# A fused attention and FFN kernel on one core: the order table of its steps, its engine lists and its buffer slots laid out anew

## The chip, the core and the metric

The kernel runs on one core of a Trainium2 chip. Five instruction streams run beside each other and meet through semaphores: PE (TensorE, matrix products), DVE (VectorE), ACT (ScalarE), POOL (GpSimd) and SP (SyncE, which here only issues DMAs). Each works through its own instructions in order. The metric is the device time of one launch in microseconds; a shorter time is better.

## What is computed

Two blocks follow each other. The first is a polynomial-sketch attention over 4 batches, 4 heads, 1088 positions and head size 32; the second is a multiplicative feed-forward block on the 4352 rows of 128 that come out of it.

```
phi(x):  a = x @ S1.T ; b = x @ S2.T            # 8 + 8 features
         phi = outer(a, b) flattened            # 64 features
kv  = sum_s phi(k)[s] v[s] ;  z = sum_s phi(k)[s]
x   = (phi(q) @ kv) / (phi(q) @ z + 1e-6)       # heads side by side: 4352 x 128
h   = ((x @ w1) * (x @ w2)) @ w3                # 4352 x 1024
out = h @ w_out                                 # 4352 x 128, float32
```

The four weights arrive as float64 and are put together from their 32-bit words on the chip. The kernel never forms `h`: it multiplies `w3 @ w_out` once (`w3o`, 1024 x 128) and computes `out = ((x@w1)*(x@w2)) @ w3o`.

## The kernel before

The kernel is a set of 1179 named steps, each a few lines that issue one to sixty-four instructions. A table, `ORDER`, names every step once, and the program is recorded in that order; so each engine's queue is `ORDER` with the steps of the other engines taken out. Three more tables belong to it: `POOL` names the steps whose elementwise work goes to POOL instead of DVE, `CPV` the copies that go to DVE instead of ACT, and `SLOTS` says for five kinds of buffers which slot each new tile takes (`b`: the eight PSUM banks). A tile that takes a slot again waits for the last reader of the tile that held it.

The steps by name, with the lines of the profile:

- `s.*`: the sketch matrices. `s.Pp` (L409 to L412) makes three 32x32 blocks of their squares.
- `k0.*` to `k3.*`, one per batch: `lead`/`rest` split the keys into a leading and a lower part (ACT L211, L212 or DVE; L651), `gram0` to `gram4` form the 32x32 Gram matrices (PE, L659: 72 fp32 products per batch, four heads on four column strips of the array), `T`, `N` (L883 to L912) turn these into the denominator's factors, `kv` (L769) sums phi(k) v, `kp` makes phi(k) (L677).
- `q0`, `q1`, `q2`, `q3`, `q4`, `q6`, `qr`: one group of query rows each. For `q0`: `sma`, `sta`, `sha`, `sla`, `sca` and the same with `y` (L1074, L201, L204, L1097, L1101) split small products into a high and a low part, `al` (L1170) adds them up, `p01`, `p2`, `p12`, `dn`, `de`, `rc` make the reciprocal of the denominator, `phi0`, `phi1` (L1208) the features, `x0`, `x1` the product with kv, `xs`, `xt` spread the reciprocal, `xT0`, `xT1` (L1291) give the first group of 512 columns of `x` transposed. `q1.sm`, `st`, `sh`, `sl`, `Ct` are the next group's split (L1137, L201, L204, L1157, L1130).
- `w0` to `w10`: eleven blocks of 1 MB of weights: `load` (SP), `c` and `m` (ACT), `j` (DVE), `a0`, `a1` (POOL). `f0` to `f7`: `t` (DVE) and `m` (PE, L534) build `w3o`.
- `g0` to `g3`: the FFN on groups of 512 columns. For each of eight slices `c`: `a` and `b` (PE, L1799 and L1809, 128x128 times 128x512), `c` (a copy out of PSUM), `m` (DVE, the product), `o` (PE, L1835).
- `h4` and `h6`: groups 4 and 5, and 6 and 7, as a seven-product Strassen-like scheme. `h4.0a1` to `h4.3b7` (PE, L1673) use half the rows of the array each: `a` steps rows 0 to 63, `b` steps rows 64 to 127. `h4.0P1` to `h4.3P7` (PE, L1759) use half the columns each. `m`, `T`, `k` are the elementwise steps around them.
- `gr`: the last 256 columns, with `a`, `b` as above (256 columns wide) and `o` (L1824, 128 wide). `g0.oT` and `g0.st` and their like turn a result and store it (four DMAs on SP).

What sets the order of the work is thus `ORDER` alone, with the waits of data and of slots. `UNDER_WAY` lets a bulk load start only when the bulk load four before it has landed.

Of the kernel before, what the change touches and what calls it, by code (L numbers as in the profile page):

```python
# [78 lines left out]
k1.zero s.Pm warm5 q0.l1 q0.A0 warm6 kr0.ab k0.lead1 q0.rm q0.sma q0.sta warm7 k0.kT0 v0.load v0.loadr k1.load k0.ab1  # L79
q0.sha k0.rest1 q0.C0 k0.gram1 k0.gram2 k0.gram3 k0.gram4 k0.ab0 k0.abc1 q1.max q0.C0t q0.sla q1.l2 k1.loadr s.Pp  # L80
k0.Gm k0.Gt k0.Ga w1.c1 k0.Gb k0.abc0 k0.T0 q1.l1 warm8 kr0.abc k0.kp1 q0.sca w1.j1 k0.Ta k0.kp0 k0.Gc w1.c0 k1.tr0
kr1.load k2.zero k1.tr1 k1.kT1 kr0.kp warm9 k0.N0 warm10 k0.Na warm11 k0.T1 k0.kv0 k0.Tc k0.Tb k0.N1 k0.Nb k0.Nh q1.rm
q0.al k0.Nf q0.phi0 q0.phi1 q0.A1 q0.smy w1.m1 k1.max q0.sty q0.shy k0.kv3 k0.kv1 k0.kv2 q0.sly s.KS k0.kvr kr1.tr
k0.kvm w1.m0 kr1.kT q0.p01 q1.C0 q1.C1 q0.C1 k0.kzt k2.loadr q0.pt0 q0.C1t q0.scy q0.p2 k0.kz q0.pt1 k0.kvc kr1.ab
k0.kqt q0.p12 q0.dn q0.de q0.rc w1.j0 q0.pc0 q0.pc1 q0.x0 k1.kT0 q0.x1 q0.xs0 q0.xs1 q0.xt0 w1.a0 q1.A0 k2.load
w0.load k1.lead0 q0.xc0 q0.xc1 k0.kq w1.a1 k2.max q0.xt1 k1.ab q0.xT0 q0.xT1 g0.4a q1.load g0.5a q1.sm w0.m1 q1.st
# [1848 lines left out]
```

## Time and profile before

| | |
|---|---|
| time of one launch, median of 3 runs | 245.70 us (245.46 to 246.02) |
| span of the profiled execution, first to last instruction | 244.1 us |
| what lies around the span, by the median | 1.6 us |
| granted TensorE clock over the span | 0.998 |
| HBM read and written | 19.40 MB and 2.23 MB |

The profiled execution has no launch time of its own beside its span, so the 1.6 us between the span and the median stands for what lies around it.

The profile is read by engine: a row of a timeline gives the start, the length, the engine, the line of the kernel, the operation, output and inputs, and in square brackets how long the engine stood idle before it and what ended that. A row for a stretch of time gives each engine's busy time in it with the number of instructions, the granted clock and the DMA share. PE and PEld are the products and the weight loads of one and the same engine. An fp32 product leaves two records of products and two of weight loads, a transposition one of each.

### The profile page before, as it was taken

Reading aid. Unit: us, or ns where it says so; the run is one execution under the profiler, and the core shown is the slowest. Engines: PE = TensorE matmul, PEld = TensorE weight load, DVE = VectorE, ACT = ScalarE, POOL = GpSimd, SP = SyncE. Lnnn points to the kernel's source line nnn. Section 1 sums busy time; section 2 is a strip of 40 time slices with the busy share of each in tenths; the row PEclk is TensorE's granted clock in tenths of the full one; section 3 lists DMA queues with packets and bytes.
Section 4 is the critical chain, followed back from the end, with each engine's and each line's share of the span. In section 5 each row is a group of like instructions: output and inputs, shape, how many; then the busy total and the mean of one; then the engine's idle time right before and its main releaser. Section 6 shows DMA issues by size and latency. Waiting matters only on the chain.

```text
span 244.1 us, 6745 instructions
## 1 busy us (share of the span) xinstructions
PE 236.2 (97%) x2724; PEld 129.8 (53%) x2724; DVE 206.7 (85%) x421; ACT 123.5 (51%) x246; POOL 161.9 (66%) x203
## 2 busy tenths in 40 slices
...
GB/s 201 265 143 325 181 227 190 6 197 224 220 141 251 188 217 190 59 1 3 3 0 0 4 0 3 59 113 3 1 0 0 0 3 0 0 1 3 12 90 93
DMA packets 31935, 22.06 MB, mean 90 GB/s; under 512 B 21280, under 2 KB 26528, under 8 KB 31904
## 3 DMA queue, kind: packets, MB, share of 16 engines
...
q8 instruction: 21, 0.34, 0.6%
...
HBM read 19.40 MB, written 2.23 MB: 89 GB/s over the span
## 4 chain that ended last, share of the span: by engine, by line
PE 87%; DMA 5%; ACT 2%; POOL 2%; DVE 1%; issue 1%; POOLq 0%; SPq 0%
PE b_ps L1809 12%; PE ps_o L1835 12%; PE ps_X L1673 11%; PE a_ps L1799 11%; PE ps_o L1759 10%; PE ps_w3o L534 6%; PE ps_Y L1673 6%; PE ps_Z L1673 3%; PE ps_g L659 2%; PE ps_x L1527 2%; PE ps_ac L1374 2%; DMA qh<-in_q_dram 2%; DMA k<-in_k_dram 2%; PE ps_or L1824 2%; POOL ph L1208 1%; PE idle_ps L255 1%
## 5 line engine op out<-in xcount | busy, mean ns | idle before, releaser
L1673 PE MATMUL ps_X<-xd,wv 64*128 64x512 f32 x112 | 36.3, 593 | 0.0
L1799 PE MATMUL a_ps<-xT,w 128*128 128x512 f32 (+1 forms) x80 | 36.1, 562 | 0.0
L1809 PE MATMUL b_ps<-xT,w 128*128 128x512 f32 (+1 forms) x80 | 35.6, 555 | 0.0
L1804 ACT COPY ffa<-a_ps 128x512 f32<-128x512 f32 (+1 forms) x38 | 20.1, 540 | 29.2 <-PE a_ps L1799 26.7
L1707 POOL TENSOR_TENSOR hc<-hc 128x512 f32<-128x512 f32 x16 | 20.7, 1304 | 15.7 <-DVE hc L1685 15.5
L1835 PE MATMUL ps_o<-ab,w3o 128*128 128x512 f32 x64 | 29.6, 600 | 0.0
L1680 ACT COPY hc<-ps_X 128x512 f32<-128x512 f32 x38 | 21.3, 590 | 16.1 <-PE ps_X L1673 12.9
L1815 DVE TENSOR_TENSOR ab<-ffa,b_ps 128x512 f32<-128x512 f32 (+1 forms) x40 | 23.9, 623 | 4.9 <-PE b_ps L1809 4.1
L501 POOL TENSOR_TENSOR w3c<-w3c,cv_m 128x512 int32<-128x512 int32 x16 | 21.2, 1344 | 4.2 <-DVE w3c L495 4.1
L1673 PEld LDWEIGHTS ps_X<-xd,wv 64*128 64x128 f32 x112 | 14.9, 186 | 13.1 <-issue 10.9
L1799 PEld LDWEIGHTS a_ps<-xT,w 128*128 128x128 f32 x80 | 14.1, 189 | 13.9 <-issue 8.8
L1809 PEld LDWEIGHTS b_ps<-xT,w 128*128 128x128 f32 x80 | 14.4, 190 | 13.1 <-issue 8.1
L1673 PE MATMUL ps_Y<-xd,wv 64*128 64x512 f32 x48 | 19.7, 594 | 0.0
L1835 PEld LDWEIGHTS ps_o<-ab,w3o 128*128 128x128 f32 x64 | 11.6, 190 | 13.4 <-issue 13.0
L534 PEld LDWEIGHTS ps_w3o<-wo,w3T 128*128 128x128 f32 x128 | 15.3, 192 | 2.4 <-issue 2.4
L534 PE MATMUL ps_w3o<-wo,w3T 128*128 128x128 f32 x128 | 15.7, 276 | 0.0
L1759 PE MATMUL ps_o<-hc,w3o 128*64 128x512 f32 x32 | 15.1, 595 | 0.0
L1759 PE MATMUL ps_o<-tt,ws 128*64 128x512 f32 x32 | 13.7, 594 | 0.0
L1680 ACT COPY hc<-ps_Y 128x512 f32<-128x512 f32 x14 | 8.1, 592 | 9.7 <-PE ps_Y L1673 6.6
L263 ACT ACTIVATE cv_c<-raw 128x1024 f32<-128x1024 f32 (+1 forms) x13 | 13.0, 1014 | 0.0
L1540 ACT COPY xd<-ps_x 64x256 f32<-64x256 f32 x24 | 8.8, 367 | 7.2 <-PE ps_o L1835 6.8
...
## 6 DMA issues: line engine op xcount, KB each, us to landing
...
```

What stands on the lines that cost most here:

```text
L263: act.activation(dst, hi.bitcast(F32), ACT.Prelu, scale=2.0 ** -112, alpha=-2.0 ** 32)
L501: pool.tensor_tensor(d, d, x["m"][:, i * 512:(i + 1) * 512], ALU.add)
L534: pe.matmul(t["o"], w3T[ko][:, c], wo[:, c], start=c == 0, stop=c == NC - 1)
L1673: pe.matmul(x[bank], stat(j, u)[:, i * 128:(i + 1) * 128], rows(j, u), start=new, stop=True, tile_position=(u * 64, 0), skip_group_check=True)
L1680: cp(n(y))(x[k], x[bank])
L1707: on(f"h{g}.{i}m{k}").tensor_mul(both[0][k], both[0][k], both[1][k])
L1759: pe.matmul(acc_o[bank][half[0]:half[1]], w(i), x(i), start=n == 1, stop=n == (2 if j == 3 else 4), tile_position=(0, half[0]), skip_group ...
L1799: pe.matmul(x["a"][:, :w], w_of(0, c), xT[g][:, c0:c0 + w], start=True, stop=True)
L1804: cp(f"g{g}.{c}{su}c")(x["s"][:, :w], x["a"][:, :w])
L1809: pe.matmul(x["b"][:, :w], w_of(1, c), xT[g][:, c0:c0 + w], start=True, stop=True)
L1815: dve.tensor_mul(ab_sb[g, c][:, c0:c0 + w], x["s"][:, :w], x["b"][:, :w])
L1835: pe.matmul(o_ps[g], w3o[:, c], ab_sb[g, c], start=n == 1, stop=n == NC)
```

## The change

All code below the tables is the same; the tables `ORDER`, `SLOTS`, `POOL` and `CPV` are replaced, so every step still runs once and issues what it issued. Of the 1179 steps the first 60 stand as they stood (to `q0.sma`); behind them the order is another one. The steps in `POOL` rise from 90 to 97 (27 leave it, 34 come to it), those in `CPV` from 17 to 21. One table line more moves every line below by one (L1673 becomes L1674).

```diff
 POOL = set("""
...
-    h6.1m22 h6.2T1 h6.2T4 h6.2m11 h6.3T3 h6.3m11 h6.s1 h6.s2 h6.s4 k0.Nf k0.Nh k0.Nr k0.kp1 k1.Nr
-    k1.kp1 k2.kp0 k2.kp1 k2.rest0 k3.kp0 k3.kp1 q0.al q0.p01 q0.phi1 q0.sca q1.al q1.bs q1.p12
...
-    qr.p12 qr.p2 s.KS s.Pp s.blk s.blkh s.low s.rest
...
+    k0.Nr k0.kp1 k1.Nr k1.kp0 k1.kp1 k2.Nr k2.kp0 k2.kp1 k2.rest0 k3.Nr k3.kp0 k3.rest0 q0.p01
+    q0.p12 q0.phi0 q0.phi1 q1.al q1.bs q1.p12 q1.p2 q1.phi q1.sca q1.scy q2.bs q2.p12 q2.sl q3.al
...
 ORDER = """
...
-h4.0ah h4.1bc h4.0b6 h4.0be h4.0a6 h4.s4 h4.0ae h4.0bh h4.1a6 h4.1b6 h4.1be h4.0b3 h4.1ad h4.1ae h4.0a5 h4.0ad g1.st
...
+h4.1a1 g2.oT h4.0b1 o.S4 qr.xT0 g1.oT h4.0a1 h4.s3 h4.0ac o.S3 h4.0b5 h4.0a2 h4.0b2 h4.s2 h4.1a5 h4.1ac h4.s4 h4.0a6
+h4.1a6 h4.0bc h4.0b6 h4.0ah h4.1b1 h4.0bd h4.0bh h4.0be v.4 h4.1ae h4.0b3 h4.0ae h4.0a5 h4.0b7 h4.1ad h4.0a7 h4.0ad
```

Among the steps of `h4` and `h6`, those of the form `h4.0a2` or `h4.0b2` are PE's half products: `a` on rows 0 to 63 of the array, `b` on rows 64 to 127. Before, a run of one half is one or two long, and wherever the 112 of them are cut into pairs from the start of a stretch, each pair holds one of each half. Now the table has runs of three as well: from `h4.0a2` on it reads a, b, a, a, a, b, b, b. In the column halves of `h6` there are two such runs.

Three places, row by row. First DVE, from the split of the low sums of `q0` (the first row, `s_t<-s_gy`, is `q0.sty`) to the first columns of `x`. Before:

```order
L201 SCALAR_TENSOR_TENSOR s_t<-s_gy,ps_ay 128x128
L204 SCALAR_TENSOR_TENSOR s_hiy<-s_gy,s_t 128x128
L1097 TENSOR_TENSOR s_loy<-ps_ay,s_hiy 128x128
L1068 STREAM_TRANSPOSE ay_C_601<-ps_cy 128x128
L1101 TENSOR_TENSOR s_loy<-s_loy,ay_C_601 128x128
L1180 TENSOR_TENSOR s_pr<-s_al,s_loy 128x128
L1184 TENSOR_TENSOR s_pr<-s_pr 128x128
L1189 TENSOR_REDUCE s_d<-s_pr 128x2x16
L1194 SCALAR_TENSOR_TENSOR s_rc<-s_d 128x16
L1198 RECIPROCAL s_rc<-s_rc 128x16
L466 TENSOR_SCALAR w_81<-cv_c 128x2x256
L1274 COPY xc<-ps_xt 128x256 x2
```

Of the change, where `s_g`, `s_t_598`, `s_hl` and `ay_C<-ps_c` are the split of `q1`:

```order
L202 SCALAR_TENSOR_TENSOR s_t<-s_gy,ps_ay 128x128
L202 SCALAR_TENSOR_TENSOR s_t_598<-s_g,ps_a 128x256
L205 SCALAR_TENSOR_TENSOR s_hiy<-s_gy,s_t 128x128
L205 SCALAR_TENSOR_TENSOR s_hl<-s_g,s_t_598 128x2x128
L1069 STREAM_TRANSPOSE ay_C_606<-ps_cy 128x128
L1098 TENSOR_TENSOR s_loy<-ps_ay,s_hiy 128x128
L1102 TENSOR_TENSOR s_loy<-s_loy,ay_C_606 128x128
L1181 TENSOR_TENSOR s_pr<-s_al,s_loy 128x128
L1158 TENSOR_TENSOR s_hl<-ps_a,s_hl 128x2x128
L1131 STREAM_TRANSPOSE ay_C<-ps_c 128x384
L1190 TENSOR_REDUCE s_d<-s_pr 128x2x16
L1195 SCALAR_TENSOR_TENSOR s_rc<-s_d 128x16
```

The split of `q1` moved ahead of the reciprocal of `q0`, into the places between its steps; `q0.p12` (L1184) left for POOL.

Second PE, between the Gram matrices of batch 1 and those of batch 2 (`ps_T`, `ps_N` are `k1.T`, `k1.N`, `ps_ph` the transpositions of `q1.pt`, `ps_x` is `q1.x`). Before:

```order
L1799 MATMUL a_ps<-xT,w_81 128x512
L889 MATMUL ps_T<-RS,G_a 32x32
L890 MATMUL ps_T<-RS,G_c 32x32
L891 MATMUL ps_T<-RS,G_b 32x32
L1246 MATMUL ps_ph<-ident,ph 128x128 x4
L1799 MATMUL a_ps<-xT,w_81 128x512 x2
L1809 MATMUL b_ps<-xT,w_81 128x512
L1246 MATMUL ps_ph<-ident,ph 128x128 x4
L1809 MATMUL b_ps<-xT,w_81 128x512
L912 MATMUL ps_N<-T_p,P2a 32x8 x4
L912 MATMUL ps_N<-T_p,P2b 32x8 x4
L912 MATMUL ps_N<-T_p,P2s 32x8 x8
```

Of the change, from `k2.ab` (`ps_ab`) on:

```order
L728 MATMUL ps_ab<-kT,KS 32x256 x8
L913 MATMUL ps_N<-T_p,P2a 32x8 x4
L913 MATMUL ps_N<-T_p,P2b 32x8 x4
L913 MATMUL ps_N<-T_p,P2s 32x8 x8
L1247 MATMUL ps_ph<-ident,ph 128x128 x4
L1800 MATMUL a_ps<-xT,w_81 128x512 x2
L1247 MATMUL ps_ph<-ident,ph 128x128 x4
L1810 MATMUL b_ps<-xT,w_81 128x512
L1298 MATMUL ps_x<-pT,kz_658 64x512 x2
```

Before, `k1.N` is followed by `q1.x` and at once by 72 Gram products; now the transpositions and three products of `g0` stand between `k1.N` and them, and `k2.ab` has come ahead of both.

Third PE, from the last column-half products of `h6` to the last products of all. Before:

```order
L1824 MATMUL ps_or<-w3o,ab 128x128 x3
L1759 MATMUL ps_o<-hc,ws 64x512 x2
L1824 MATMUL ps_or<-w3o,ab 128x128
L1799 MATMUL a_ps<-xT,w_81 128x256
L1809 MATMUL b_ps<-xT,w_81 128x256
L1759 MATMUL ps_o<-hc,ws 64x512 x2
L1799 MATMUL a_ps<-xT,w_81 128x256
L1824 MATMUL ps_or<-w3o,ab 128x128
L1809 MATMUL b_ps<-xT,w_81 128x256 x3
L1799 MATMUL a_ps<-xT,w_81 128x256
L1824 MATMUL ps_or<-w3o,ab 128x128
L1809 MATMUL b_ps<-xT,w_81 128x256
```

Of the change:

```order
L1760 MATMUL ps_o<-tt,w3o 64x512
L1810 MATMUL b_ps<-xT,w_81 128x256
L1800 MATMUL a_ps<-xT,w_81 128x256
L1825 MATMUL ps_or<-w3o,ab 128x128 x2
L1800 MATMUL a_ps<-xT,w_81 128x256
L1825 MATMUL ps_or<-w3o,ab 128x128
L1800 MATMUL a_ps<-xT,w_81 128x256
L1810 MATMUL b_ps<-xT,w_81 128x256 x2
L1825 MATMUL ps_or<-w3o,ab 128x128
L1810 MATMUL b_ps<-xT,w_81 128x256 x2
L1825 MATMUL ps_or<-w3o,ab 128x128 x12
```

All column-half products (L1759, now L1760) now stand in one piece ahead of `gr`'s products; before, two pairs of them stood among these, and one pair of row halves (L1673) between six products of `gr` and the first column halves.

More of the change, by code (lines that the diff above doesn't have):

```diff
@@ L78 @@
 warm3 s.rest w1.load s.T s.P s.tc warm4 q0.l2 k0.kT1 s.Pc s.R k0.g k0.lead0 s.c s.blk k0.rest0 q1.tr k0.gram0 s.blkh
[L79 to L86, printed above, removed]
-q1.Ct g0.4c g0.4b q1.sh q1.sl k1.rest0 g0.7b w0.c1 g0.7a k1.abt w0.j1 k1.gram0 w0.c0 s.RC q1.scy k1.gram1 kh2.load
@@ L98 @@
-q2.x q2.load k2.N0 k2.Tb k3.lead0 w9.a1 k2.N1 g1.4b q3.al q3.p2 q3.p12 q2.xT0 g2.5a k3.kT1 g2.5c g2.6a q3.dn q3.de
-k2.Na g1.3m g2.4a g2.3a w5.m g2.4b g2.6c k3.rest0 g1.0b k2.Nr q3.rc g1.1m g1.4m g1.6b k2.Nb g0.2b kr1.kp w6.j q4.tr
-g2.4c g1.6m w7.load w7.c q3.bs q4.max q2.restT w6.m w5.j w2.j q4.l2 w3.load w9.a0 k3.gram0 k3.gram1 k3.gram2 q3.load
-w7.j q3.phi0 k3.gram3 k3.gram4 g2.2a k3.Gc g2.1a g1.0m w2.a0 g2.6b g2.0a g2.4m g2.1c f6.t w6.a0 w4.load g2.3b w2.a1
-g2.2b g2.2c g2.0c w6.a1 g2.1b q3.pT0 k3.Gm g0.2m k3.Gt k3.kT0 v3.load w7.m f6.m w5.a1 w5.a0 g2.3c k3.Ga k3.Gb g2.3m
@@ L138 @@
[L138 to L142 removed]
+k1.zero s.Pm warm5 q0.l1 q0.A0 warm6 kr0.ab k0.lead1 q0.rm q0.sma v0.load k0.ab1 s.Pp q0.C0 k0.gram1 kr0.abc k0.kT0
@@ new lines @@
+q0.sta q1.max kr1.load q0.sha k0.rest1 kr1.tr k0.abc1 k0.ab0 k0.gram2 k0.gram3 k1.load q0.C0t q1.l2 k0.gram4 q0.sla
+k1.loadr k1.tr1 w0.load k0.Gm q1.l1 warm7 warm9 q0.sca kr0.kp k0.Gt k0.Ga k0.Gc k0.kp1 q0.al k0.T0 k1.max k2.zero
+k0.Gb k0.Ta k0.T1 k0.Tc k2.loadr k0.Tb kr1.kT k1.tr0 k0.N0 k0.abc0 q1.rm k0.Na w1.m1 s.KS k0.N1 q0.phi0 k1.kT1 k0.Nh
+w1.c0 w1.m0 warm10 q0.pt0 q0.A1 k1.kT0 warm11 kr1.ab q1.A0 k0.Nb v0.loadr k0.Nf q1.C0 k0.kp0 q0.smy k0.kv0 k0.kv3
+w0.c0 q0.C1 k0.kv1 q1.C1 w1.c1 w6.load w0.m0 q1.sm q0.sty w0.c1 q1.st q0.shy q1.sh q0.phi1 q0.C1t kh2.load k0.kv2
```

143 lines of the change are left out of this document (76 added, 67 removed).

## The prediction

> **What bounds the kernel now.** I read the page's engine line first, then the busy time by stage, then the chain that ended last.
>
> ```profile
> span 244.1 us, 6745 instructions
> PE 236.2 (97%) x2724; PEld 129.8 (53%) x2724; DVE 206.7 (85%) x421; ACT 123.5 (51%) x246; POOL 161.9 (66%) x203
> ```
> ```profile
> core 0: us, PE busy (x) PEld busy (x) DVE busy (x) ACT busy (x) POOL busy (x), PEclk, DMA share, GB/s
> 15.00:27.42 12.42, 11.17 (x256) 8.63 (x256) 9.99 (x34) 9.26 (x22) 6.83 (x11) 1.00 0.68 215
> 27.42:49.10 21.68, 20.28 (x454) 10.99 (x454) 19.12 (x46) 15.05 (x30) 13.60 (x18) 1.00 0.63 152
> 49.10:155.70 106.60, 106.60 (x1369) 59.60 (x1364) 94.21 (x196) 56.24 (x108) 76.12 (x67) 1.00 0.39 97
> 155.70:240.60 84.90, 84.86 (x401) 39.63 (x400) 75.11 (x122) 33.03 (x63) 56.96 (x69) 1.00 0.14 24
> ```
>
> The second column of numbers is PE. From 49.10 to 240.60 us it is never idle (106.60 of 106.60, 84.86 of 84.90), and the clock column stands at 1.00. There an order can only win by giving PE less to do between its products, and can lose by making PE wait. Up to 49 us PE does wait: 1.40 us in the row that starts at 27.42, and more before it, where it fills its time with idle products. The share of 97% hides this. So three places are worked out: the start of the first FFN product, the waits up to 49 us, and the joints between kinds of products later.
>
> The joints can be read in the chain of the last stretch (start, length, line, records).
>
> ```profile
> 218.99 0.43 PE b_ps L1809 x2
> 219.42 1.06 PE ps_X L1673 x4
> 220.48 10.45 PE ps_o L1759 x48
> 230.93 0.87 PE ps_or L1824 x6
> 231.79 1.01 PE ps_o L1759 x4
> 232.80 0.42 PE ps_or L1824 x2
> 233.22 0.43 PE a_ps L1799 x2
> 233.65 0.43 PE b_ps L1809 x2
> 234.09 1.01 PE ps_o L1759 x4
> 235.09 0.63 PE a_ps L1799 x2
> ```
>
> A product 256 wide on the whole array takes 0.43, so one 512 wide takes 0.86. A pair of half products, four records, would take 0.86 too: 48 records are 12 pairs or 10.32, and the row says 10.45. But a pair alone takes 1.06 or 1.01, the single 128-wide product 0.42 instead of 0.22, the whole product after a pair 0.63 instead of 0.43. Each change between row halves, column halves and the whole array costs 0.15 to 0.20 us.
>
> **Term 1, the first FFN product.** It waits for the first columns of x, the last of a DVE row.
>
> ```profile
> 27.42 1.10 PE L1799 MATMUL a_ps<-xT,w 128*128 128x512 f32 x2
> ```
> ```profile
> 19.64 0.78 DVE L1208 TENSOR_TENSOR ph<-s_al,s_bs 128x512 f32<-128x512 f32 x1
> ...
> 23.20 0.32 DVE L1068 STREAM_TRANSPOSE ay_C<-ps_cy 128x128 f32<-128x128 f32 x1 [1.38 <-PE ps_cy L1030]
> ...
> 24.28 0.29 DVE L1184 TENSOR_TENSOR s_pr<-s_pr 128x128 f32<-128x128 f32 x1
> ```
> ```profile
> 26.48 0.79 DVE L1291 TENSOR_TENSOR xT<-xc,ps_xs 128x256 f32<-128x256 f32 x2
> 27.19 0.42 DVE L1137 TENSOR_REDUCE s_g<-ps_a 128x32 f32<-128x256 f32 x1
> ...
> 27.98 0.57 DVE L1130 STREAM_TRANSPOSE ay_C<-ps_c 128x384 f32<-128x384 f32 x1
> ...
> 28.92 0.42 DVE L1157 TENSOR_TENSOR s_hl<-ps_a,s_hl 128x256 f32<-128x256 f32 x1
> ```
>
> Ahead of x, DVE now also does the five steps of q1's split, which ended at 29.34: four of about 0.42 and one of 0.57, 2.25 in all. From POOL come q0.sca and q0.al (about 0.29 each, like the like-sized row at 24.28) and s.Pp, four operations on 32 partitions. Their DVE price is not shown; rows of 32x32 on DVE take 0.17 to 0.18, so 0.7, between nothing (if they fall in a wait) and 2.1, their four rows on POOL. q0.phi0 (0.78) and q0.p12 (0.29) leave DVE. That is 2.25 + 0.58 + 0.7 - 1.07 = 2.5 more. Cover is there: DVE was busy 9.99 of the 12.42 us before the product, 1.38 of the rest in the one wait at 23.20. I put the part not hidden at 0.3, with -0.4 (q1's split wholly in waits) and +0.9 (the cover gone because POOL, which now runs both halves of q0's features, one after the other, is late) as ends. The four w0 and w1 conversions that ACT now does before x lie in its waits (9.26 busy of 12.42). **+0.3.**
>
> **Term 2, up to 49 us.** Three waits of PE are put down to "issue", no data:
>
> ```profile
> 14.27 0.22 PE L659 MATMUL ps_g<-k,kk 128*32 128x32 f32 x1 [0.41 <-issue]
> ```
> ```profile
> 20.35 0.26 PE L769 MATMUL ps_kv<-kp,v 128*32 128x64 f32 x4 [0.91 <-issue]
> ```
> ```profile
> 46.98 0.19 PE L659 MATMUL ps_g<-k,kk 128*32 128x32 f32 x1 [1.16 <-issue]
> ```
> ```profile
> 14.26:20.34 6.08, 5.17 (x124) 4.26 (x125) 4.78 (x17) 4.49 (x11) 4.12 (x8) 1.00 0.58 186
> 20.34:46.98 26.64, 24.90 (x505) 14.51 (x505) 22.59 (x61) 19.87 (x41) 15.60 (x19) 1.00 0.70 183
> ```
> ```profile
> q8 instruction: 21, 0.34, 0.6%
> ```
>
> Between the first two waits PE ran 124 products and 125 weight loads, with its own waits on semaphores some 256 instructions; between the second and third 1010, four times that. The instruction queue moved 21 packets, 0.34 MB, 16 KB each: one per 256 of PE's 5448 records. So PE stalls where it reaches the end of a block of instructions before the next one has come. The third block began at k1.N, near 43.1, and the next was there at 46.98: 3.9 us. Gram products run at 13 ns per instruction and burn a block in half of that.
>
> Counted in the new order (four instructions an fp32 product, two a transposition), the same limit, 1474 instructions in, falls in k1.N again, but three whole products, eight transpositions and q1.x now stand in that block ahead of the Gram products: some 6 us, more than 3.9. The wait of 1.16 goes. The limits at 450 and 706 fall in k0.gram3 and at the end of q1.C0; a stall there, up to the 0.91 of before, is in term 1's upper end.
>
> The Trainium skill, page "Runtime: NRT & Kernel Launch", section "Instruction fetch mechanics", says that refills come in 16 KiB blocks of 256 instructions, and that fetch is hidden behind issue. The block size agrees with the 21 packets; that it is hidden does not, by the 1.16 us. By that rule term 2 would be +0.1.
>
> What is late next: of the rest of PE's idle time (1.40 - 1.16 = 0.24) I keep nothing. New waits come at q1.x, for ACT, and at the second Gram matrix, for a PSUM bank that the copy g0.2c now frees on DVE. From x to that copy DVE has 36 instructions; at the mean of the row at 27.42 (19.12 / 46 = 0.416) 15.0 us, and 1.5 more to wait for k1.lead0 on ACT. PE reaches it after the same products as before (16.8 us from the first) plus k2.ab (0.5): 17.3. The margin is thin, so I charge 0.4 for both. 0.4 - 1.40 is **-1.0**, with -1.4 and +0.8 (both waits at 1.1) as ends.
>
> **Term 3, the joints.** From the start of h6's column halves the old order changes between halves and the whole array eight times (rows, whole, rows, columns, whole, columns, whole, columns, whole); the new one three times (rows, whole, columns, whole). Five at 0.15 to 0.20: **-0.8**, ends -1.0 and -0.5. The joints of h4 are four in both. Whether POOL or DVE does an m or a T of h4 and h6 costs nothing while PE is covered by the rows from 155.70 on: DVE 75.11 of 84.90, POOL 56.96. Without cover each DVE step moved (the k steps' rows are 0.69) would show whole. The last DMAs are as before: the final store needs the last product, and four stores' issue hides beside gr's products.
>
> **Sum.** 245.7 (244.1 of span and 1.6 around it, which is also the median of the runs) + 0.3 - 1.0 - 0.8 = **244.2 us**.
>
> **Rivals.** (a) *The halves do not run apart.* In the old order each successive pair of half products holds one of each half; the new one has runs of three. If a half product must wait until the one before it in the program has started, "a a a b b b" leaves the other half empty: counted over the 168 half products, 89 slots of 0.86 instead of 84, +4.3. With the sum: 248.5. It decides from one pair that doesn't match. Against it:
>
> ```profile
> 74.58 0.34 PE L659 MATMUL ps_g<-kk 128*32 128x64 f32 x8
> 74.72 0.25 PE L659 MATMUL ps_g<-k,kk 128*32 128x32 f32 x7
> ```
>
> The program has a product of the first kind and one of the second for each head in turn, on four column strips; the trace starts the first kind of all four heads (eight records) before the second. So strips pass each other by at least three products. That is shown for columns, not for row halves. The Trainium skill, page "TensorE: Matmul & The Clock Gate", section "Part 3: Packing small matmuls — row/col tiling", says that matmuls start and end strictly in program order; by that rule this rival's time would hold, and the rows at 74.58 speak against it. 10%.
>
> (b) *Another engine binds after x.* DVE's work by g0.2c slips, q1.x and the Gram products wait 2 us instead of 0.4, and the later order, with no slack to give back, keeps it: 244.2 + 1.6 + 0.9 (term 1's upper end less 0.3, and a stall at a block's end) = 246.7, slower. It decides from a DVE delay of 1 us at x. For it: DVE is busy 19.12 of 21.68. 13%.
>
> (c) *The change does not do what it says.* The halves were already full (84 slots for 168), so following them apart gains nothing, the joints are hidden by weight loads, and term 1 and 2 cancel: 245.7, no change. 15%.
>
> **How the numbers follow.** The forecast, 243.2 to 245.1, has 59%; 3% lie lower, since all lower ends together give -0.4 - 1.4 - 1.0, 242.9. 10% (a), 13% (b), 15% (c). About 0.2%, 0.5 us, is what a measurement of this kernel can tell from no change. Faster: 62%. Same: 15%. Slower: 23%. The range takes in (b) and (c) and leaves out (a) and the rest below: 242.9 to 247.0.
>
> **What would show it.** Term 1: the first row of L1800 starts near 27.7. Term 2: no issue wait near the second Gram matrix, and q2.C1 ends near 48.4 instead of 49.1. Term 3: one uninterrupted row of column halves for h6, followed only by gr's products. Rival (a): gaps of 0.43 or 0.86 inside one half of L1674. Rival (b): PE idle behind DVE before 50 us. The forecast is wrong if PE is idle anywhere between 50 and 235 us.

## The result and the profile after

The changed kernel takes 248.80 us (median of 4 runs, 247.79 to 249.27) against 245.58 us (245.22 to 246.02) for the kernel before on the same chip: a ratio of 1.0139, 95% interval 1.0108 to 1.0169. In a second set of runs it took 249.99 us against 245.42, a ratio of 1.0159 (1.0103 to 1.0214). It is slower by 1.0 to 2.1%; 244.2 had been forecast. Its runs also lie further apart: 247.76 to 250.63 over both sets. A ratio is worked out from all runs of both kernels, so it need not be that of the two medians; one run each of e1, e2 and e7, over 1.5% above the fastest of its kernel, is left out of it.

The profiled execution is the fastest of the first four (247.79 us, span 245.8). The page's first lines, and the busy times in the four stretches that the rest of this text uses: up to the first FFN product, from there to the end of `q2.C1`, from there to the first row half of `h4`, and from there to the last product. The second column of numbers is PE.

```profile
span 245.8 us, 6748 instructions
PE 238.4 (97%) x2724; PEld 139.3 (57%) x2724; DVE 209.1 (85%) x421; ACT 118.8 (48%) x242; POOL 157.0 (64%) x207
```
```profile
core 0: us, PE busy (x) PEld busy (x) DVE busy (x) ACT busy (x) POOL busy (x), PEclk, DMA share, GB/s
15.00:27.87 12.87, 11.36 (x329) 8.71 (x329) 10.89 (x38) 10.87 (x26) 8.38 (x16) 1.00 0.72 192
27.87:48.41 20.54, 20.54 (x455) 11.15 (x455) 17.64 (x45) 15.56 (x29) 15.09 (x16) 1.00 0.96 236
48.41:155.84 107.43, 106.91 (x1366) 59.33 (x1366) 93.28 (x187) 51.21 (x100) 70.11 (x66) 1.00 0.34 83
155.84:242.24 86.40, 86.38 (x405) 49.41 (x400) 78.26 (x125) 31.14 (x65) 57.14 (x75) 1.00 0.13 21
```

The second stretch looks as forecast: PE is never idle in it. But the third, in which the kernel before had no idle PE at all, now has 0.52 us of it, and the fourth is 1.5 us longer with PE called busy all the time. "Busy" hides it: a single row half at work counts as PE busy. The end of the chain shows the order that was announced, one row of column halves for `h6` and only gr's products behind it:

```profile
222.24 12.43 PE ps_o L1760 x56
234.66 0.63 PE b_ps L1810 x2
...
239.26 2.97 PE ps_or L1825 x24
```

Since a kernel's executions differ, the same four stretches were read from every profile, at the same rows. All columns are in us (the first counts from the start of the span); the experiments in the table follow below.

| profile | first FFN product | to the end of q2.C1 | to the first row half | to the end of the last product |
|---|---|---|---|---|
| before | 27.42 | 21.75 | 106.54 | 84.85 |
| order of before: e6 | 26.13 | 21.79 | 106.55 | 84.61 |
| order of before: e8 | 27.05 | 21.46 | 106.53 | 90.62 |
| order of before: e9 | 26.21 | 22.81 | 105.93 | 84.61 |
| changed | 27.87 | 20.54 | 107.43 | 86.38 |
| changed, second profile (e0) | 28.87 | 22.04 | 107.97 | 86.37 |
| e1 | 28.29 | 20.83 | 106.71 | 86.39 |
| e2 | 27.42 | 20.74 | 110.57 | 85.53 |
| e3 | 27.68 | 20.35 | 107.74 | 86.22 |
| e4 | 27.26 | 21.87 | 106.49 | 85.52 |
| e7 | 27.54 | 20.94 | 107.66 | 84.85 |
| e10 | 27.00 | 26.98 | 108.19 | 86.40 |
| e11 | 28.08 | 21.45 | 106.48 | 85.51 |
| e12 | 29.07 | 21.25 | 108.16 | 85.52 |

Over the profiles whose edit leaves a stretch untouched, the change costs +1.48 in the first (mean 28.18 of the changed one, e0, e1, e2, e3, e11, e12 against 26.70 of before, e6, e8, e9), -0.68 in the second (20.99 against 21.67 of before, e6, e8), +0.9 to +4.0 in the third (the changed one, e0, e2 and e3, mean +1.9; +1.2 without e2) and +1.53 in the fourth. That is +3.5 to +4.2, and the two sets of runs gave +3.2 and +4.6.

### The profile page after: what moved, and what is told of

Read it like the earlier page. It is cut to its first block, busy times and chain, and to the rows that moved or that the text cites. A ratio compares the mean times of both kernels' runs of the same rounds, so it can differ in the third digit from the quotient of the medians.

```text
span 245.8 us, 6748 instructions
## 1 busy us (share of the span) xinstructions
PE 238.4 (97%) x2724; PEld 139.3 (57%) x2724; DVE 209.1 (85%) x421; ACT 118.8 (48%) x242; POOL 157.0 (64%) x207
## 4 chain that ended last, share of the span: by engine, by line
PE 82%; DMA 6%; DVE 6%; POOL 2%; SPq 1%; issue 1%; DVEq 0%
PE ps_X L1674 12%; PE ps_o L1836 11%; PE a_ps L1800 11%; PE b_ps L1810 11%; PE ps_o L1760 10%; PE ps_w3o L535 6%; PE ps_Y L1674 6%; DMA qh<-in_q_dram 4%; PE ps_Z L1674 3%; DMA kr<-in_k_dram 3%; PE ps_ac L1375 2%; PE ps_x L1528 2%; PE ps_g L660 2%; PE ps_or L1825 2%; POOL w3c L502 1%; PE ps_kv L770 1%
## 5 line engine op out<-in xcount | busy, mean ns | idle before, releaser
L1674 PE MATMUL ps_X<-xd,wv 64*128 64x512 f32 x112 | 39.9, 597 | 0.0
L1810 PE MATMUL b_ps<-xT,w 128*128 128x512 f32 (+1 forms) x80 | 36.3, 558 | 0.5 <-DVE ab L1816 0.5
L1800 PE MATMUL a_ps<-xT,w 128*128 128x512 f32 (+1 forms) x80 | 36.1, 557 | 0.2 <-DVE xT L1292 0.2
L1805 ACT COPY ffa<-a_ps 128x512 f32<-128x512 f32 (+1 forms) x34 | 17.4, 535 | 30.4 <-PE a_ps L1800 29.3
L1681 ACT COPY hc<-ps_X 128x512 f32<-128x512 f32 x35 | 19.9, 596 | 18.8 <-PE ps_X L1674 16.7
L1674 PE MATMUL ps_Y<-xd,wv 64*128 64x512 f32 x48 | 23.5, 594 | 0.0
L1674 PEld LDWEIGHTS ps_X<-xd,wv 64*128 64x128 f32 x112 | 17.5, 186 | 9.7 <-issue 5.3
L1800 PEld LDWEIGHTS a_ps<-xT,w 128*128 128x128 f32 x80 | 14.2, 190 | 13.7 <-issue 8.1
L1708 POOL TENSOR_TENSOR hc<-hc 128x512 f32<-128x512 f32 x13 | 16.8, 1305 | 7.6 <-DVE hc L1686 7.5
L1836 PEld LDWEIGHTS ps_o<-ab,w3o 128*128 128x128 f32 x64 | 11.7, 190 | 13.8 <-issue 13.4
L1541 ACT COPY xd<-ps_x 64x256 f32<-64x256 f32 x28 | 10.3, 366 | 9.9 <-PE ps_x L1528 9.5
L1760 PE MATMUL ps_o<-hc,ws 128*64 128x512 f32 x32 | 14.8, 595 | 0.0
L1760 PE MATMUL ps_o<-hc,w3o 128*64 128x512 f32 x32 | 14.5, 595 | 0.0
L264 ACT ACTIVATE cv_c<-raw 128x1024 f32<-128x1024 f32 (+1 forms) x13 | 13.0, 1012 | 1.9 <-DMA raw<-in_moe_w_dram 1.6
L1743 POOL TENSOR_TENSOR tt<-tt,hc 128x512 f32<-128x512 f32 x4 | 5.9, 1482 | 11.7 <-DVE hc L1708 7.8
L1760 PE MATMUL ps_o<-tt,ws 128*64 128x512 f32 x32 | 13.2, 594 | 0.0
```

The costliest lines, as they stand in the source:

```text
L264: act.activation(dst, hi.bitcast(F32), ACT.Prelu, scale=2.0 ** -112, alpha=-2.0 ** 32)
L1674: pe.matmul(x[bank], stat(j, u)[:, i * 128:(i + 1) * 128], rows(j, u), start=new, stop=True, tile_position=(u * 64, 0), skip_group_check=True)
L1681: cp(n(y))(x[k], x[bank])
L1708: on(f"h{g}.{i}m{k}").tensor_mul(both[0][k], both[0][k], both[1][k])
L1760: pe.matmul(acc_o[bank][half[0]:half[1]], w(i), x(i), start=n == 1, stop=n == (2 if j == 3 else 4), tile_position=(0, half[0]), skip_group ...
L1800: pe.matmul(x["a"][:, :w], w_of(0, c), xT[g][:, c0:c0 + w], start=True, stop=True)
```

## The experiments

Lines in kernels that keep the old tables' length are one lower (L1673 for L1674, L1799 for L1800). In the diffs the table is cut to the steps that move.

**e0: the changed kernel again.**

> The changed kernel once more, for a second profile: its profiled run (span 245.8 us) was the shortest of four, the others had 246.8 to 247.4. Theory W (what was lost hangs on waits, one of them on when a DMA lands): the rows up to 155 us move between the two profiles, the row of b_ps near 77.7 us with its wait for DVE above all, and the last product ends up to 1.5 us later than 242.2. Rival O (the order of the half products itself loses): rows up to 155 us agree within 0.2 us and the difference lies behind 155 us.

This profile has a span of 248.8 us, 3.0 more than the first, and the last product ends 3.0 later. All of it lies ahead of 81 us. In the timeline of PE (start, length, and in brackets how long PE stood idle before and what ended that), and in that of ACT for the row with L264:

```profile
16.30 0.19 PE L660 MATMUL ps_g<-k,kk 128*32 128x32 f32 x1 [0.93 <-issue]
```
```profile
41.91 0.24 PE L913 MATMUL ps_N<-T_p,P2a 32*32 32x8 f32 x8 [0.81 <-ACT krab L835]
42.59 0.24 PE L913 MATMUL ps_N<-T_p,P2s 32*32 32x8 f32 x8 [0.30 <-ACT T_p L909]
```
```profile
40.61 1.15 ACT L264 ACTIVATE cv_c<-raw 128x1024 f32<-128x1024 f32 x1 [3.06 <-DMA raw<-in_moe_w_dram]
```
```profile
80.72 0.70 PE L1810 MATMUL b_ps<-xT,w 128*128 128x512 f32 x1 [1.07 <-DVE ab L1816]
```

ACT stood 3.06 us at `w9.c`, for a load; `kr1.abc` and `k1.Tc` queue behind it, and PE's `k1.N0` and `k1.N1` behind those. The wait at b_ps is twice that of the first profile. From 81 us on the distance of the two profiles stays the same within 0.15 us, so the time of the runs varies with what lies ahead of 81. The rows up to 155 us do move, as theory W said; that the end moves by 3.0 us is twice what it allowed. The last DMA of the load that ACT stood for took 3.5 us from issue to landing in both profiles. It was issued later here (37.06 against 34.69), since by `UNDER_WAY` it waits for the landing of `q1.load`, and that took 9.1 us against 7.4.

**e1: one reader of a DMA later.** In the first profile of the change DVE's row and SP's issue show where the wait at b_ps comes from:

```profile
70.46 0.35 SPq L976 DMA_DIRECT2D qh<-in_q_dram  x1
```
```profile
73.08 1.18 DVE L1451 SCALAR_TENSOR_TENSOR s_rc<-s_d 128x16 f32<-128x16 f32 x1
75.91 0.25 DVE L980 STREAM_TRANSPOSE qT_rest<-qh 128x64 f32<-128x64 f32 x1 [1.65 <-DMA qh<-in_q_dram]
...
76.94 0.68 DVE L1816 TENSOR_TENSOR ab<-ffa,b_ps 128x512 f32<-128x512 f32 x1
```
```profile
77.68 1.55 PE L1810 MATMUL b_ps<-xT,w 128*128 128x512 f32 x3 [0.52 <-DVE ab L1816]
```

DVE reaches `q3.restT` at 74.26, 3.8 us after the issue of `q3.load`, and stands until it has landed; the product `g1.7m` (76.94) that frees PE's bank stands behind it. In the table of before `q3.restT` stood 97 steps behind its load, now 17; in time, 13.4 us behind its issue (61.06 to 74.44) without a wait, now 3.8.

```diff
-q3.restT k3.gram0 q3.rc w2.j k3.gram1 qr.max k3.gram2
+k3.gram0 q3.rc w2.j k3.gram1 k3.gram2
...
-g1.7m k3.abt g2.2b f6.t
+g1.7m k3.abt g2.2b f6.t q3.restT
...
-q3.phi0 w4.c q3.pT0
+q3.phi0 w4.c qr.max q3.pT0
```

> The change, but DVE's step q3.restT and ACT's qr.max, which read the rows of q that q3.load brings, stand some 5 us later in the table (behind f6.t and behind w4.c); all else as in the change. Theory W: DVE no longer stands 1.65 us at q3.restT (74.26 to 75.91), g1.7m is done in time and PE's wait of 0.52 us at b_ps (77.68) goes; the row halves of h4 start about 0.5 us earlier than 155.84, and the time falls by 0.5 to 1.5 us (more if the landing is later in runs without a profile) to 247.3 to 248.3. Rival: another product waits instead, since PE has no slack to win there; time as the change's, 248.8.

247.84 us (246.31 to 250.07), ratio 1.0084 (1.0043 to 1.0124), 2.15 below the change in the same set and 0.96 below it in the first; the intervals of the two ratios still touch. The wait at b_ps is gone, and the third stretch is 106.71, within 0.2 of before's. Theory W's sign came; its 0.5 to 1.5 us can't be told from a little more. The wait differs between executions, 0.52 in the first profile, 1.07 in e0, 0.83 in e3, 2.32 in e2, and it costs more than the idle time of PE: the third stretch is longer by 0.89, 1.43 and 1.20 in the first three.

**e2: four banks.** In the rows of `h4` one half runs alone. PE's first rows there, and ACT's:

```profile
155.84 1.12 PE L1674 MATMUL ps_Y<-xd,wv 64*128 64x512 f32 x2
156.94 0.69 PE L1674 MATMUL ps_X<-xd,w 64*128 64x512 f32 x1
156.94 0.69 PE L1674 MATMUL ps_X<-xd,wv 64*128 64x512 f32 x1
...
159.62 1.02 PE L1674 MATMUL ps_Y<-xd,wv 64*128 64x512 f32 x2
```
```profile
152.34 4.55 ACT L1541 COPY xd<-ps_x 64x256 f32<-64x256 f32 x12 [2.41 <-PE ps_x L1528]
156.91 0.62 ACT L1550 COPY xT<-ps_x 128x64 f32<-128x64 f32 x4
```

`h4.1b5` starts at 155.84 alone. `h4.1a1` takes the bank that ACT's last copy of `q6.x` reads until 156.89 (152.34 + 4.55), and starts at 156.94. At 159.62 the a half runs a whole product alone: the next b product, `h4.0b6`, stands behind two a products that have not started, and it starts beside the first of them (e8 takes up how far a half product reaches).

```diff
-h4.1b5 h4.1a1 g2.oT h4.0b1 o.S4 qr.xT0 g1.oT h4.0a1
+h4.1b5 g2.oT h4.1a1 g1.oT h4.0b1 o.S4 qr.xT0 h4.0a1
...
+# slots of "b" from h4.1a1 on: 1 -> 2, 2 -> 7, 3 -> 1, 7 -> 3
```

> The change with the same queues on all engines; from h4.1a1 on four PSUM banks trade names (1 to 2, 2 to 7, 3 to 1, 7 to 3), so that h4.1a1 takes the bank that g2.oT has read out by 155.87 us instead of the one that ACT's q6.xT2 reads out until 156.88. Theory W: h4.1b5 and h4.1a1 run beside each other from 155.9, no half runs alone for 1.1 us, and no slot of 0.86 stays empty near 160.5; the rows of h4 (28.14 us) fall to 26.9 to 27.4, the time by 0.7 to 1.2 us to about 247.8. Rival O (half products start in the order of the program, so a a a b b b leaves the other half empty): the gap of 0.86 near 160.5 stays, rows of h4 at 27.8 or more, time within 0.4 us of 248.8.

The two halves start 0.09 apart, and the rows take 186.03 - 158.73 = 27.30 instead of 28.14; the empty slot is down to a gap of 0.26. So 0.85 of the fourth stretch was the bank: with the same runs of three in the queue and both halves started together, the slot is not lost. The time (249.00, ratio 1.0117, 1.0064 to 1.0170) doesn't show it and misses theory W's 247.8; this profile has the longest wait at b_ps of all and a new effect behind it. Its rows, and the busy times with the granted clock (the column after POOL):

```profile
158.73 0.69 PE L1673 MATMUL ps_Y<-xd,wv 64*128 64x512 f32 x1
158.82 0.69 PE L1673 MATMUL ps_X<-xd,w 64*128 64x512 f32 x1
```
```profile
79.23 4.25 PE L1809 MATMUL b_ps<-xT,w 128*128 128x512 f32 x6 [2.32 <-DVE ab L1815]
```
```profile
76.90:79.20 2.30, 0.01 (x1) 0.00 (x0) 1.75 (x6) 1.41 (x3) 0.67 (x1) 1.00 0.35 90
79.20:80.90 1.70, 1.67 (x4) 0.86 (x5) 1.70 (x3) 1.70 (x4) 1.70 (x2) 0.89 0.00 1
80.90:83.90 3.00, 3.00 (x5) 1.15 (x4) 3.00 (x6) 1.88 (x3) 2.17 (x3) 0.50 0.22 70
```

Behind the idle 2.32 us the clock stands at half for 3.4 us (0.4 of the second row and all of the third), which costs another 1.7. With the wait that is the 4.0 by which the third stretch of this profile is longer.

**e3: the new order up to 155 us, the old one behind.**

```diff
 # ORDER of the change up to and with qr.x; the other steps as in ORDER, POOL and CPV of before
```

> The changed table up to and with qr.x (155 us), from there the steps in the order and on the engines of the kernel before; buffer slots of the rest laid out for this order. Theory W with the loss behind 155 us: the stretch from the row halves on takes 84.9 us as before and the time is 245.7 to 246.5. If the loss of the unprofiled runs lies ahead of 155 us (a DMA that lands late): 246.8 to 247.5. Rival O gives the same as the first here; that the new order up to 155 us is the gain that was forecast would give 245.0 or less.

247.69 us (246.91 to 249.40), ratio 1.0099 (1.0065 to 1.0133): above every number that was expected. With the old pairs of halves the rows still take 183.95 - 155.76 = 28.19, and a product at their start waits for ACT:

```profile
155.76 1.12 PE L1673 MATMUL ps_Y<-xd,wv 64*128 64x512 f32 x2
157.15 0.69 PE L1673 MATMUL ps_Y<-xd,wv 64*128 64x512 f32 x1 [0.27 <-ACT xT L1549]
```

So the rows lose their time to what precedes them. In the change `q6.x` runs at 150.85 and in the kernel before at 145.38; ACT's copies of it and of `qr.x` end at 157.53 instead of 153.6, when PE already stands at the rows. Theory W had put that loss behind 155 us; its cause lies ahead of it.

**e4, e11, e12: waits taken out together.** e11 is e1 and e2; e4 adds two moves, e12 another.

```diff
 # e4, beside e1 and e2
-w9.c kr1.abc g0.4m g0.3a k2.ab k2.lead0 q2.max k1.Tc k2.abt g0.3c
+kr1.abc g0.4m g0.3a k2.ab k2.lead0 q2.max k1.Tc k2.abt g0.3c w9.c
-kr1.tr k0.abc1 k0.ab0 k0.gram2
+k0.abc1 k0.ab0 k0.gram2
...
-k1.loadr k1.tr1 w0.load
+k1.loadr k1.tr1 w0.load kr1.tr
 # e12, beside e1 and e2: w9.c as in e4, and w9.m, w5.load behind q1.pc1
```

> The change with four of its waits taken out by moving steps or banks, nothing else: q3.restT and qr.max some 5 us later (as in e1_restT_later), the four banks traded at h4.1a1 (as in e2_banks), w9.c (ACT's conversion that stood waiting for its load for 1.6 and 3.1 us in the two profiles, with k1.N0 on PE behind it) moved behind g0.3c, kr1.tr moved behind k1.tr1 on PE. Theory W (the loss is waits on landings of DMAs, and the bank of q6.xT2): against the change -0.5 to -1.5 at b_ps, -0.85 in the rows of h4, 0 to -1.1 near 40 us; kr1.tr's wait of 0.6 may only be traded for one on issue. Time 245.5 to 247.0, the rows of h4 at 27.3, and the runs lie closer together than 247.8 to 250.6. Rival (the new order is dense: what is taken out at one place is lost at the next): 247.8 or more.

> The change with only e1_restT_later's and e2_banks' edits together (q3.restT and qr.max later, four banks traded at h4.1a1). Theory W: of what the change loses behind 49 us, the wait at b_ps (0.5 to 2.3 us, more where it drops the clock) and 0.85 us in the rows of h4 are gone, so the stretch from q2.C1's end to the rows is 106.5 to 106.8 and from the rows to the end 85.5 us; what is left against the kernel before is the first product (1.2 us later on the mean) less 0.8 up to q2.C1, plus 0.7 in the rows and the tail: 0.6 to 1.4 us over before, 246.0 to 246.9. Rival (dense order, other waits grow): 247.5 or more.

> As e11_two_waits_out, and ACT's w9.c behind g0.3c, w9.m and the load w5.load that waits for it behind q1.pc1, so that neither kr1.abc, k1.Tc, q1.pc0, q1.pc1 nor g0.1c stands behind the landing of w9.load. In e4_waits_out w9.c alone was moved, w9.m stayed ahead of q1.pc0 and q1.x's products took 1.1 us longer. If ACT's place behind that load costs PE time: the stretch from the first FFN product to q2.C1's end falls to 20.3 to 20.6 (20.5 and 22.0 in the two profiles of the change, 21.9 in e4), and the time to 245.4 to 246.3, with runs closer together. If w5.load's later start makes a conversion late: no gain, or a loss of up to 1 us behind 50 us.

e4: 246.53 us (245.71 to 247.52), ratio 1.0044 (1.0023 to 1.0066). e11: 246.95 (245.63 to 247.61), 1.0057 (1.0037 to 1.0078). The third stretch is 106.49 and 106.48, as before's to 0.1 us; the fourth 85.5; the spread of the runs is under 2 us. So two waits hold some 60% of the loss. e4 lies in the range of its theory W, e11 at the upper end of its own. What is left in e11, 1.4 us by its ratio, is the later first product (28.08 against 26.70 on the mean) and 0.66 in the fourth stretch, less 0.2 in the second. The second stretch of e4 is 21.87: `q1.x` took 1.1 us longer, with `q1.pc1` now behind `w9.c` and `w9.m` on ACT. e12 was to mend that, and is a miss: 247.43 (246.27 to 249.90), 1.0086 (1.0050 to 1.0123). Its second stretch is 21.25, its third 108.16. With `w5.load` issued later, a load of v behind it on SP is now waited for directly:

```profile
63.82 0.43 PE L769 MATMUL ps_kv<-kp,v 128*32 128x64 f32 x16 [1.44 <-DMA v<-in_v_dram]
```

**e6: the joints alone**, in the kernel before.

```diff
-h6.2P4 g4.oT h6.2P2 gr.3o1 h6.k1 gr.2o0 gr.2o1 h6.2P3 h6.k3
+h6.2P4 g4.oT h6.2P2 h6.2P3 h6.0P3 h6.3P3 h6.1P3 gr.3o1 h6.k1 gr.2o0 gr.2o1 h6.k3
...
-g4.oS h6.k2 h6.k4 h6.0P3 gr.7o0 g4.st gr.0a gr.5b h6.k5 h6.k6 h6.3P3 h6.1P3 h6.k7
+g4.oS h6.k2 h6.k4 gr.7o0 g4.st gr.0a gr.5b h6.k5 h6.k6 h6.k7
```

> The kernel before, but the two pairs of column halves h6.2P3, h6.0P3 and h6.3P3, h6.1P3 stand in one piece with the other column halves instead of among the products of gr: four joints fewer, as in the change. As forecast (each joint is worth 0.15 to 0.20): the last product ends 0.6 to 0.8 earlier counted from the start of the column halves, the time falls by as much. Theory W (what is saved on PE there is lost again in waits for DVE, whose chain k1 to k9, oT and gr's products is as long as before): 0 to 0.3 us, and PE shows new waits for DVE's ab among the last products of gr.

245.12 us (244.41 to 246.65), ratio 1.0000 (0.9979 to 1.0021); the fourth stretch gains 0.24. The chain that ended last now leaves PE behind the column halves:

```profile
219.23 10.47 PE ps_o L1759 x48
229.73 0.69 DVE oc L1776
230.44 0.70 DVE oc L1780
...
234.69 0.69 DVE oc L1785
235.40 0.71 DVE oT L1842
236.47 2.62 PE ps_or L1824 x20
```

Behind the column halves DVE does nine steps of 0.7 one after the other (`k2`, `k4` to `k9`, two `oT`) and then gr's elementwise products, for which PE's last ten products (20 records) wait. The products that stood between the halves had filled that time. Counted from the start of the first column half (219.16, before 220.41), PE reaches its last ten products after 17.31 us instead of 17.75, so it saves 0.44 with the four joints, and these products then take 0.22 longer. In the change that same stretch, from the first column half of `h6` to the last product, is 20.05 us against 20.15; its column halves, with two runs of three, take 12.43 where `h4`'s in the kernel before take 12.17.

**e7: the front of the new order alone.**

```diff
 # ORDER of the change up to and with q2.Ct (w9.c and kr1.tr moved as in e4); the other steps as before
```

> The changed order only up to q2.Ct (49 us), with w9.c and kr1.tr moved as in e4_waits_out; from there the steps in the order and on the engines of the kernel before, with slots laid out for it. If the forecast's term 2 holds (no issue wait at the second Gram matrix) and nothing is given back later: the second row of ps_ac ends 0.5 to 0.8 us earlier than before's 49.10 and the time is 244.6 to 245.2. If the front of the new order is no better on the average (its first product was at 27.4, 27.7, 27.9, 28.3 and 28.9 in five profiles): 245.4 to 246.5. If slots that the rest finds taken make it wait: more.

246.94 us (246.04 to 254.70), ratio 1.0066 (1.0036 to 1.0096). The second stretch is 0.8 shorter, but the first is no better than 27.54, and the third loses 1.1 of its own at the seam. So it gives no support to the front, and it came out where the expectation put it if slots make the rest wait; how much the seam hides is open.

**e8: runs of three alone**, in PE's queue of the kernel before. One of the six places:

```diff
-h4.0b4 h4.0a4 h6.s2 h4.1bh h4.2b1 h4.0ai h4.1a7 h4.0af h4.1b7 h4.2a1
+h4.0a4 h6.s2 h4.1bh h4.0ai h4.1a7 h4.0af h4.2a1 h4.0b4 h4.2b1 h4.1b7
```

> The kernel before, with PE's queue alone changed: in six places of the row halves of h4 and h6 three pairs a b a b a b (in any order within a pair) are written a a a b b b. Counted in slots of 0.86 for the two stretches of row halves (56 as it was): rival O, strict program order (a product starts only when the one before it has started), 67 slots, so 9.4 us more; a product may pass one that has not started, 58 slots, 1.7 us more; it may pass two or more, 56 slots, within 0.3 us of before. Theory W (the rows of h4 lost their time to a bank, not to the runs of three) needs one of the last two.

251.56 us (251.01 to 251.65), ratio 1.0242 (1.0216 to 1.0267), +6.1 us: between the counts of 9.4 and 1.7. The rows of `h4` take 29.61 instead of 26.82 and those of `h6` 23.60 instead of 20.80. How far a half product reaches is read best in the third of the six places, where the queue holds `h4.2a4`, `h4.3a3`, `h6.0a1`, then `h4.2b4`:

```profile
178.00 0.59 PE L1673 MATMUL ps_Y<-xd,wv 64*128 64x512 f32 x1
178.00 1.45 PE L1673 MATMUL ps_X<-xd,wv 64*128 64x512 f32 x3
179.29 0.59 PE L1673 MATMUL ps_Y<-xd,wv 64*128 64x512 f32 x1
179.29 0.69 PE L1673 MATMUL ps_X<-xd,wv 64*128 64x512 f32 x1
...
180.15 0.59 PE L1673 MATMUL ps_X<-xd,w 64*128 64x512 f32 x1
```

The first row ends the b half's `h4.3b5`; the two later records of the second are `h4.2a4`, from 178.43. At 179.29 `h4.3a3` (ps_Y) and `h4.2b4` (ps_X) start together, and `h6.0a1`, the only one with w as its weights, follows at 180.15. So `h4.2b4` has passed `h6.0a1`: strict order is out. But it did not start beside `h4.2a4`, where its half was free. Nothing shown held it there: it waits for no semaphore, and DVE's product whose end frees the bank of `h6.0a1` ended at 178.83. So a half product passes one that has not started, and not two: free passing is out too. The fifth and sixth places read the same way (210.16 and 217.41).

In the first place a second thing shows. The queue holds `h4.0a4`, `h4.1a7`, `h4.2a1`, then `h4.0b4`; `h4.0b4` starts at 164.80, not beside `h4.1a7` at 164.63. `h4.2a1`, ahead of it, waits for DVE's product that ends at 164.74, so it seems that a product's wait also holds the next one of the other half; the fourth place fits that (203.38, behind an end at 203.31). The 1.7 counted for a reach of one counted queue positions alone. A delayed b half is also late for DVE, whose row then comes late to the next a half, again in the first place:

```profile
166.64 0.69 DVE L1712 TENSOR_TENSOR hc<-hc,ps_X 128x512 f32<-128x512 f32 x1 [1.90 <-PE ps_X L1673]
167.25 1.27 DVE L1685 TENSOR_TENSOR hc<-hc,ps_X 128x512 f32<-128x512 f32 x2
```
```profile
167.98 0.69 PE L1673 MATMUL ps_X<-xd,wv 64*128 64x512 f32 x1 [0.34 <-DVE hc L1685]
168.01 0.69 PE L1673 MATMUL ps_Z<-xd,w 64*128 64x512 f32 x1
```

At such a wait both halves start again together, so the next run of three can cost its slot anew. As an estimate, six slots of 0.86 are 5.2 of the 6.1 us.

**e9: the issue wait alone**, in the kernel before with e6's edit.

```diff
-k2.gram0 g0.1m k2.gram1 k2.gram2 q3.max k2.gram3 g0.0c k2.kT0 k1.Nb q1.xT k2.gram4 q3.l2 k2.ab q2.A0 q2.C0 q2.C1
-q3.l1 k1.kp0 v1.zero w9.c k2.abt g1.5a g1.5c g1.1a q2.Ct g1.7a
+k2.gram0 g0.1m k2.gram1 q3.max q1.xT g1.5a k2.gram2 g1.5c q3.l2 g1.1a k2.gram3 g0.0c k2.kT0 k1.Nb k2.gram4 g1.1c
+k2.ab q2.A0 q2.C0 q2.C1 q3.l1 k1.kp0 v1.zero w9.c k2.abt q2.Ct g1.7a
```

> The kernel before with two edits: the column halves of h6 in one piece (as in e6_before_columns_in_one, where the stretch behind the row halves' start gained 0.24 us), and the first two products of g1 (g1.5a, g1.1a, with ACT's copies of them) moved from behind q2.C1 into the second Gram matrix, one behind k2.gram1 and one behind k2.gram2. No engine gets more work. If PE stands in the second Gram matrix because its next block of 256 instructions has not come (3.26, 3.55 and 2.94 us for 1.82 us of products in three profiles of this order), two whole products (1.7 us of work in 8 instructions) give the fetch its time: no issue wait there, the stretch from the first FFN product to the end of q2.C1 and two products later shrinks by 1.0 to 1.5 us, time 243.9 to 244.5. Rival: the stall is not the fetch but DVE or ACT behind it, and comes back at the next product that waits for them: 245.1, as e6.

245.42 us (244.65 to 246.50), ratio 1.0001 (0.9981 to 1.0020). No issue wait is left in the second Gram matrix, so it was the block that had not come. The counts agree: in all fourteen profiles each issue wait of 0.1 us or more stands behind 449 or 450, 705, 961, 1729 or 1986 records of products and weight loads, steps of 256 or a multiple of it. But the gain is given back at the next product:

```profile
49.77 1.12 PE L1799 MATMUL a_ps<-xT,w 128*128 128x512 f32 x2 [0.76 <-DVE ay_C L1391]
```

PE now waits 0.76 for DVE (`q2.At`), and pays 0.20 at each of the two products set between Gram rows (1.06 from one start to the next kind's for 0.86). From the first FFN product to the row halves the whole takes 128.74, against 128.29 in the kernel before. The forecast had the cause of the stall, the rival the time: the issue wait had covered a wait for DVE.

**e10: the split of q1 behind x again**, in the change.

```diff
-q0.C1 k0.kv1 q1.C1 w1.c1 w6.load w0.m0 q1.sm q0.sty w0.c1 q1.st q0.shy q1.sh q0.phi1
+q0.C1 k0.kv1 q1.C1 w1.c1 w6.load w0.m0 q0.sty w0.c1 q0.shy q0.phi1
...
-k1.ab w0.m1 q0.xT0 g0.5a
+k1.ab w0.m1 q0.xT0 g0.5a q1.sm q1.st q1.sh q1.sl q1.Ct q1.sca
```

> The change, but DVE's split of q1 (q1.sm, q1.st, q1.sh, q1.sl, q1.Ct, 2.25 us, with POOL's q1.sca) stands behind the first columns of x again, where it stood before; slots laid out for it. Theory F (the first FFN product of the change is set by DVE's row, in which these steps are not hidden; in the kernel before it was set by PE's two issue waits, 0.41 and 0.91 in its first profile and less in the others): the first FFN product starts at 26.3 to 27.0 instead of 27.4 to 28.9. As forecast in term 1 (0.3 of them not hidden): 27.1 to 28.6. In both cases what follows has that DVE work to do then, and the stretch to q2.C1 (20.4 to 22.0 us) is longer by up to as much.

```profile
27.00 1.96 PE L1799 MATMUL a_ps<-xT,w 128*128 128x512 f32 x4 [0.22 <-DVE xT L1291]
32.50 1.22 PE L1799 MATMUL a_ps<-xT,w 128*128 128x512 f32 x1 [3.54 <-POOL w L470]
```

The first product starts at 27.00, at the upper end of what theory F gave and outside what the forecast gave, but still up to 0.9 behind the profiles of the old order. It is one profile, and the seven of the changed front scatter from 27.42 to 29.07. The rest of the run (253.48 us, ratio 1.0329, 1.0296 to 1.0362) is another matter: on POOL `q1.sca` now waits for DVE's split with a conversion of weights behind it, and PE stands 3.54 us for that.

## Why the prediction was wrong

**The step that failed** is the one that was not there. The sum had three terms, and none between 49 and 155 us, on the ground that PE is never idle there in the kernel before, so that "an order can only win by giving PE less to do between its products, and can lose by making PE wait". The second half of that sentence was not followed up. The change's waits behind 49 us are worth +1.2 to +1.9 in the third stretch and +0.85 at the start of the fourth, more than all gains that were forecast. Against the forecast the first stretch is 1.2 us worse, the second 0.3, the third by these 1.2 to 1.9 for which there was no term, the fourth 2.3. The prediction asked of the elementwise steps that changed engine whether a row of PE covers them, but not how far a step that reads a DMA stands behind its load. 97 steps had become 17 for `q3.restT`. Its last part named the sign by which it would fall, PE idle between 50 and 235 us, and that sign came. e1, e4 and e11 show the cause of this part; taking two waits out (e11) leaves a ratio of 1.0057 of the 1.0139 and 1.0159.

**Term 1** (+0.3, first product near 27.7): 27.87 came, and `q2.C1` ended at 48.41 where 48.4 was forecast, but that was luck of one profile: over the seven of the changed front the end lies between 48.0 and 50.9. The term was wrong in its base and in its size. The 27.42 of the kernel before held two issue waits of 0.41 and 0.91, which differ from execution to execution. Here are those of e8 with the same order up to there; e6 has neither and e9 only 0.25 of the first:

```profile
14.44 0.22 PE L659 MATMUL ps_g<-k,kk 128*32 128x32 f32 x1 [0.66 <-issue]
19.98 0.69 PE L769 MATMUL ps_kv<-kp,v 128*32 128x64 f32 x34 [0.36 <-issue]
```

The new order has such waits too (0.93 in e0, 0.48 in e12). Without them the old order starts the first FFN product at 26.1 to 26.2, and the new one, in its five profiles that have none, at 27.4 to 28.3. The term was +1.48 on the mean of all, above its upper end of 0.9. e10 gets the product to 27.00 by taking DVE's split of q1 away, so part of it is DVE's row, as far as one profile can say; the rest was not taken apart. The rule of the Trainium skill that fetch is hidden (page "Runtime: NRT & Kernel Launch", section "Instruction fetch mechanics") agrees with e6 at these two places and with no profile of the old order at the second Gram matrix: 1.16, 1.45 (e6) and 0.84 (e8).

**Term 2** (-1.0): its mechanism was right and its size nearly. The stretch is 1.21 shorter in the first profile and 0.68 on the mean, and of the profiles with the new order of PE there only e12 has an issue wait in the second Gram matrix, at the same limit:

```profile
48.52 0.19 PE L659 MATMUL ps_g<-k,kk 128*32 128x32 f32 x1 [0.48 <-issue]
```

PE had passed the limit before it 7.3 us earlier, so the 3.9 us that the prediction read as a block's time is not always enough. What was missed is that a wait can stand behind this one: e9 takes it out of the old order and gains nothing, since DVE is behind it. Two slips in the working change nothing: 13 ns is the distance of two Gram records, each with its weight load (1.82 us for 144), so half of that is the time per instruction; and with fetch hidden its own terms give 0.4 - 0.24, or +0.16, where +0.1 stands.

**Term 3** (-0.8, from five joints at 0.15 to 0.20): wrong in its size, because it took a saving on PE for a saving of time. e6 takes away four of the joints and gains 0.24 of 0.6 to 0.8: PE saves 0.44, and the end of the kernel then hangs on DVE's chain of `k` and `oT` steps. In the change the same part of the kernel gains 0.1. The prediction said that a `k` step would show whole without cover, but its sum has no term for the stretch in which no rows are left.

**Rival (a)**, the halves in strict order, did not happen as described: strict order is refuted by e8. The sign given for it, a gap of 0.86 in one half, did appear, and e2 shows that it goes when the two halves start together, so the bank brought it on. A reach of one product is real, though, and e8 shows what it can cost. **Rival (b)** named the right engine and the wrong place: DVE does bind, at x and again near 77 us, the second time because it stands at a DMA. Its time, 246.7, was too low, and the one nearest to what came, 248.5, was rival (a)'s, for another reason. **Rival (c)** fell: the loss is clear of no change in both sets of runs.

What stays open: the 0.7 us by which the fourth stretch of e11 is still longer than before's, of which 0.5 lie in the rows of `h4` and 0.26 in those of `h6`; what holds the first FFN product back beside the split of q1; and why `q1.load`, on which the load for `w9.c` hangs, takes 1.7 us longer in one execution than in another.
